# An expert's last 128 tokens in a retention and mixture-of-experts kernel: first layer with the weights stationary instead of the tokens

## The chip, the cores and the metric

The kernel runs on one core of one Trainium2 chip. The metric is device time in microseconds (us) of one execution. The kernel before takes 399.38 us, the median of 3 runs (399.12 to 399.86).

## The reference

Retention attention runs over 4 sequences of 768 steps with 8 heads of 64 features. Its output is one row of 512 features for each of 3072 tokens. A gate then sends every token to one of 8 experts, and each expert is two matrix products with a relu between them.

```python
def _attn_ref(q, k, v):
    ...
    for t in range(S):
        state = gamma[None, :, None, None] * state + np.einsum('bhd,bhe->bhde', k[:, :, t], v[:, :, t])
        y[:, :, t] = scale * np.einsum('bhd,bhde->bhe', q[:, :, t], state)

def _moe_ref(x, w_gate, w1, w2):       # x: 3072 x 512, w1: 8 x 512 x 1024, w2: 8 x 1024 x 512
    ...
    for e in range(E):
        mask = expert_idx == e
        xe = x[mask]
        h = np.maximum(xe @ w1[e], 0.0)
        ye = h @ w2[e]
        out[mask] = gate_w[mask, None] * ye
```

## The kernel before, in words

**Stages.** The first part computes the retention output chunk by chunk (24 chunks of 128 tokens), gates the tokens, and scatters them into DRAM, sorted by expert. The second part, `moe_main`, goes through the experts. Expert 0 is handled in two pieces. Its first 320 tokens are computed while the last chunks of the first part still run (`early_pieces`, L793 and L812). Its last tokens, up to 128 of them, are computed in `late_block` (L899 to L960), which is the first thing in `moe_main` and the place of the change. Experts 1 to 7 follow in a loop (first layer L1009, second layer L1034 or, for the last expert, L1032), each with a fixed capacity of tokens, 452 for expert 1.

**Precision.** Every operand of an expert's product is split into a high part and a low part, both of type fp32r (`whi`, `wlo` for weights; `xh`, `xl` or the two planes of `xhl1` for tokens; `hh`, `hl` or the two planes of `hT` for the features between the layers). A product is the sum of three: high times high, low weight times high, high weight times low. So a 512 x 512 piece of first-layer weights costs 4 blocks of 128 input features (kd) times 3 products.

**A matmul's two operands.** TensorE loads one operand of up to 128 x 128, the stationary one (LDWEIGHTS, engine PEld in the profile), and then streams the other, the moving one, of up to 512 columns (MATMUL, engine PE). The output has one partition for each stationary column.

**The late block.** `hidden(i, part)` computes the first layer for half i of the 1024 features between the layers. The token block `xhl1[:, x, kd, :]` (128 x 128) is stationary and 512 weight columns move, so `hn` (PSUM) has tokens on its partitions: 12 matmuls of 512 columns for each half, in two parts of 6. ACT applies the relu into `hs` (L914). The second layer contracts over the features, so they have to lie on the partitions: `turned(i)` makes four 128 x 128 TensorE transposes into `ht` (L919), and ACT and DVE cut the result into the high and low planes of `hT` (L921, L922). `result(i, part)` is the second layer (L928): `hT` stationary, 512 columns of the second-layer weights moving, 24 matmuls summed in `pys[0]`. `put_rows` (L881) weighs the rows and POOL scatters them to the output (L738).

**What sets the order.** The scheduler is off here (`manual_schedule`): each engine runs its instructions in the order in which the code issues them. Between the steps for expert 0 the late block prepares the 452 tokens of expert 1, in four pieces j of 128 (the last of 68): `prep(j, "turn")` is a transpose on DVE (L753), "high" a cast on ACT (L760), "low" a subtraction on DVE (L767). Behind these, on ACT and DVE, stands the split of the second quarter of expert 1's weights (`split`, L132 and L133), then the fetch of the fourth quarter on SP's queue (`fetch(1, 3)`, L124, which refills a buffer freed by the split), then DVE's weighing of expert 0's first tokens (L894) and their scatters on POOL. PSUM tiles with tag "ph" come from a pool of three, shared by `hn`, `ht` and the `ph` of the later experts.

Of the kernel before, what the change touches and what calls it, by code (L numbers as in the profile page):

```python
# [9 lines left out]
F32 = mybir.dt.float32  # L10
# [3 lines left out]
AF = mybir.ActivationFunctionType  # L14
ALU = mybir.AluOpType
# [3 lines left out]
E, DM, F = 8, 512, 1024  # L19
N = B * S  # L20
P = 128
# [11 lines left out]
KD = DM // P  # L33
# [792 lines left out]
def moe_main(ctx, tc, wparts, fetch, split, xhl1, Z0, ident, buf, xg, fetch_rows, expert_at, mask7, slot_marks, natural, overflow,  # L826
             last_meta, token_index, out):
    nc = tc.nc
# [4 lines left out]
    yp = pool("yp", 2)  # L833
    ps_h = pool("ps_h", 3, space=PS)
# [14 lines left out]
    def marks(e):  # L849

        n = blocks[e]
        sidx[e], gw[e] = slot_marks[e % 3]
        nc.vector.scalar_tensor_tensor(out=sidx[e][:, 0:n], in0=xg.bitcast(I32)[:, 0:n, P], scalar=4 * ROWS,
                                       in1=mask7[:, e - 1, 0:n], op0=ALU.bitwise_and, op1=ALU.bitwise_or)
        nc.vector.tensor_copy(out=gw[e][:, 0:n], in_=xg[:, 0:n, P + 1:P + 2])

    def prep_x(e, j, engine, steps=("turn", "high", "low")):
        if "turn" in steps:
            if j == 0:
                xs[e] = [xp.tile([P, KD, CMAX], F32R, name=n) for n in ("xh", "xl")]  # L860
                if e not in natural and e > 1:
                    marks(e)
            turn_slices(nc, xt[j % 2], xg, 4 * j, widths[e][j], 0)
        args = xt[j % 2], 4 * j, widths[e][j], 0
        if "high" in steps:
            cut_high(nc, xs[e][0], *args)
        if "low" in steps:
            cut_low(nc, engine, *xs[e], *args)

    def put_rows(e, py, j):  # L870
        w = widths[e][j]
        index, meta = natural[e]
        yo = yp.tile([P, DM], F32, name="yo")

        parts = (slice(0, 2), slice(2, 4)) if e == E1 and j == len(widths[e]) - 1 else (slice(0, 4),)
        for i, k in enumerate(parts):
            args = dict(out=sliced(yo[:w, :])[:, k], in_=featured(py[:w, :])[:, k])
            if i:
                nc.scalar.activation(func=AF.Copy, scale=meta[:w, j, 1:2], **args)
            else:  # L880
                nc.vector.tensor_scalar(in0=args["in_"], out=args["out"], scalar1=meta[:w, j, 1:2], scalar2=None,  # L881
                                        op0=ALU.mult)
        scatter_rows(tc, out, index[:w, j:j + 1], yo[:w, :], "rows")
# [7 lines left out]
    def weigh(e, j):  # L891
        a, b = 4 * j, min(4 * j + 4, blocks[e])
        z = Zs[e][:, a:b].rearrange("p j k r -> p j (k r)")
        nc.vector.tensor_tensor(out=z, in0=z, in1=gw[e][:, a:b].broadcast_to([P, b - a, P]), op=ALU.mult)  # L894

    def put_slices(e, j):
        scatter_rows(tc, out_slices, sidx[e][:, j:j + 1], Zs[e][:, j].rearrange("p k r -> p (k r)"), "rows")

    def late_block():  # L899

        hs = [yp.tile([P, DM], F32, name="hs", tag="yo") for _ in range(2)]
        hT = yp.tile([P, 2, KF, P], F32R, name="hT", tag="Z")
        hn = {}

        def hidden(i, part):
            whi, wlo = wparts[0, i]
            if part == 0:
                hn[i] = ps_h.tile([P, DM], F32, name="hn", tag="ph")
            for kd in range(2 * part, 2 * part + 2):
                for n, (a, x) in enumerate(((whi, 0), (wlo, 0), (whi, 1))):  # L910
                    nc.tensor.matmul(out=hn[i], lhsT=xhl1[:, x, kd, :], rhs=a[:, kd, :],
                                     start=(kd == 0 and n == 0), stop=(kd == KD - 1 and n == 2))
            if part:
                nc.scalar.activation(out=hs[i], in_=hn[i], func=AF.Relu)  # L914

        def turned(i):
            t = ps_h.tile([P, 4, P], F32, name="ht", tag="ph")
            for j in range(4):
                nc.tensor.transpose(out=t[:, j, :], in_=hs[i][:, j * P:(j + 1) * P], identity=ident)  # L919
            hi, lo = [hT[:, n, 4 * i:4 * i + 4, :] for n in range(2)]  # L920
            nc.scalar.copy(out=hi, in_=t)  # L921
            nc.vector.tensor_tensor(out=lo, in0=t, in1=hi.bitcast(F32), op=ALU.subtract)  # L922

        def result(i, part):
            whi, wlo = wparts[0, 2 + i]
            for f in range(2 * part, 2 * part + 2):
                for n, (a, h) in enumerate(((whi, 0), (wlo, 0), (whi, 1))):
                    nc.tensor.matmul(out=pys[0], lhsT=hT[:, h, 4 * i + f, :], rhs=a[:, f, :],  # L928
                                     start=(i + f == 0 and n == 0), stop=(i == 1 and f == 3 and n == 2))

        prep = lambda j, *steps: prep_x(1, j, nc.vector, steps)
        hidden(0, 0)
        hidden(0, 1)
        prep(0, "turn")
        prep(1, "turn")
        prep(0, "high")
        prep(1, "high")
        prep(0, "low")
        hidden(1, 0)
        turned(0)  # L940
        prep(1, "low")
        prep(2, "turn")
        hidden(1, 1)
        prep(2, "high")
        result(0, 0)
        turned(1)
        prep(2, "low")
        prep(3, "turn", "high", "low")
        marks(1)
        for i in range(2):  # L950
            split(1, 1, i, nc.vector)
        fetch(1, 3)
        for j in range(-(-NJ0 // 4)):
            weigh(0, j)
        result(0, 1)
        for j in range(4):
            put_slices(0, j)
        result(1, 0)
        result(1, 1)
        put_rows(0, pys[0], 0)  # L960

    with tc.manual_schedule():

        nc.vector.memset(pys[1][:, CAPS[1]:], 0.0)
        late_block()
        for e in range(1, E):
            halves = ((0, nc.vector), (1, nc.vector))
# [5 lines left out]
            hs = []  # L973
# [29 lines left out]
            for f in range(KF):  # L1003
                fo = (f % 4) * P
                ph = ps_h.tile([P, DM], F32, name="ph")
                n = 0
                for a, x in ((0, xh), (1, xh), (0, xl)):
                    for kd in range(KD):
                        nc.tensor.matmul(out=ph[:, :cap], lhsT=wparts[e, f // 4][a][:, kd, fo:fo + P],  # L1009
                                         rhs=x[:, kd, :cap], start=(n == 0), stop=(n == 3 * KD - 1))  # L1010
# [5 lines left out]
                                               in1=hh[:, :cap].bitcast(F32), op0=ALU.max, op1=ALU.subtract)  # L1016
# [3 lines left out]
            for k in range(steps):  # L1020
# [3 lines left out]
                n = 0  # L1024
                for f in range(KF):
                    whi, wlo = wparts[e, 2 + f // 4]
                    hh, hl = hs[f]
                    for a, x in ((whi, hh), (wlo, hh), (whi, hl)):
# [4 lines left out]
                        else:  # L1033
                            nc.tensor.matmul(out=py[:, :cap], lhsT=a[:, f % 4, k * P:(k + 1) * P],  # L1034
                                             rhs=x[:, :cap], **se)
# [137 lines left out]
```

## Time and profile before

| | |
|---|---|
| median of 3 runs | 399.38 us (399.12 to 399.86) |
| the profiled execution | 400.06 us, with a span of 398.3 us from its first to its last instruction |
| mean granted TensorE clock | 0.995 |
| PE matmul instructions | 3236, busy 98% of the span |
| DVE, POOL, ACT busy | 60%, 46%, 36% |
| first matmul of the late block (L911) | 133.01 us after the start of the span |
| first matmul of expert 1 (L1009) | 145.00 us |

PE is TensorE's matmul, PEld its load of the stationary operand, DVE is VectorE, ACT ScalarE, POOL GpSimd, and SP the engine that issues most transfers. In a row of the timeline stand the start, the length, the engine, the line of the kernel, the operation, output and inputs by their names in the program, the form and the count; in square brackets how long the engine was idle before and what ended that. In a row of grouped instructions stand count, busy us, mean ns of one, and the idle time before them. Matmuls are pipelined and their ends are modelled, so the pace is read from their starts. The profile writes fp32r operands of TensorE as f32.

### The profile page before, as it was taken

What the parts mean: (1) busy time and instruction counts of PE and PEld (TensorE: products, weight loads), DVE (VectorE), ACT (ScalarE), POOL (GpSimd) and SP (SyncE); (2) the same over time, 40 slices, a digit from 0 to 9 for tenths busy, and PEclk for the clock granted to TensorE, in tenths of its full rate; (3) what the DMA queues carried; (4) which work ended last, traced back from release to release, by engine and by line L of the source; (5) the groups of instructions that cost most, each with busy time, mean ns of one, the idle gap of its engine ahead of it and who ended that gap; (6) DMA issues with size and microseconds to landing.
All of it is one profiled execution on the core that took longest, in us unless ns stands there. A gap on an engine that the chain in (4) does not pass through costs nothing. (4 is left out here: it accounts for less than half of the span.)

```text
span 398.3 us, 8240 instructions
## 1 busy us (share of the span) xinstructions
PE 390.3 (98%) x3236; PEld 356.5 (89%) x3236; DVE 240.3 (60%) x468; ACT 142.4 (36%) x249; POOL 185.2 (46%) x176
## 2 busy tenths in 40 slices
PE   8999999999999999999999999999999999999994
PEld 4888878787899889999999999999999999999972
DVE  3555757685744578573866477477737657665310
ACT  2224435224411455531542344054334416423100
POOL 1647959655260517200584077028406813740741
PEclk9999999999999999999999999999999999999998
DMA  8999999975058839547452755465564647430111
GB/s 273 422 419 420 418 416 420 324 297 149 2 216 174 327 117 305 214 167 162 166 182 92 190 183 213 84 209 165 177 152 157 234 83 232 146 133 0 54 47 48
DMA packets 42316, 81.53 MB, mean 205 GB/s; under 512 B 4444, under 2 KB 18144, under 8 KB 39844
## 3 DMA queue, kind: packets, MB, share of 16 engines
q1 hardware_dynamic: 36768, 67.46, 51.2%
q0 software_dynamic: 5360, 13.49, 9.1%
q8 instruction: 26, 0.43, 0.4%
q14 instruction: 14, 0.11, 0.1%
q10 hardware_dynamic: 148, 0.04, 0.1%
HBM read 65.90 MB, written 15.68 MB: 205 GB/s over the span
## 5 line engine op out<-in xcount | busy, mean ns | idle before, releaser
L738 POOL DMA_INDIRECT out<-Z,sidx x90 | 104.9, 1165 | 138.8 <-DVE Z L894 113.5
L133 DVE TENSOR_TENSOR wlo<-raw,whi 128x1024 fp32r<-128x1024 f32 x54 | 65.5, 1215 | 14.1 <-ACT whi L132 13.8
L132 ACT CAST whi<-raw 128x1024 fp32r<-128x1024 f32 (+1 forms) x72 | 67.3, 950 | 7.3 <-DMA raw<-w 7.3
L1034 PE MATMUL py<-hl,whi 128*128 128x452 f32 (+5 forms) x192 | 67.0, 349 | 0.0
L1034 PE MATMUL py<-hh,wlo 128*128 128x452 f32 (+5 forms) x192 | 66.8, 348 | 0.0
L1034 PE MATMUL py<-hh,whi 128*128 128x452 f32 (+5 forms) x192 | 66.8, 348 | 0.0
L1014 ACT ACTIVATE hh<-ph 128x452 fp32r<-128x452 f32 (+6 forms) x56 | 28.3, 507 | 81.5 <-PE ph L1009 81.5
L1009 PE MATMUL ph<-xh,wlo 128*128 128x452 f32 (+6 forms) x224 | 50.1, 345 | 0.0
L1009 PE MATMUL ph<-xh,whi 128*128 128x452 f32 (+6 forms) x224 | 50.1, 345 | 0.0
L1009 PE MATMUL ph<-xl,whi 128*128 128x452 f32 (+6 forms) x224 | 50.0, 345 | 0.0
L1015 DVE SCALAR_TENSOR_TENSOR hl<-ph,hh 128x452 fp32r<-128x452 f32 (+6 forms) x56 | 32.0, 574 | 29.7 <-ACT hh L1014 29.2
L1009 PEld LDWEIGHTS ph<-xh,whi 128*128 128x128 f32 x224 | 40.8, 188 | 0.8
L1009 PEld LDWEIGHTS ph<-xh,wlo 128*128 128x128 f32 x224 | 40.8, 188 | 0.8
L1009 PEld LDWEIGHTS ph<-xl,whi 128*128 128x128 f32 x224 | 40.7, 188 | 0.7
L1034 PEld LDWEIGHTS py<-hh,wlo 128*128 128x128 f32 x192 | 36.0, 188 | 0.8
L1034 PEld LDWEIGHTS py<-hl,whi 128*128 128x128 f32 x192 | 36.0, 188 | 0.7
L1034 PEld LDWEIGHTS py<-hh,whi 128*128 128x128 f32 x192 | 36.0, 188 | 0.7
L251 DVE TENSOR_TENSOR Sb<-sp,cs 128x512 f32<-128x512 f32 x48 | 30.8, 684 | 7.4 <-PE sp L248 7.4
L760 ACT CAST xh<-buf 128x512 fp32r<-128x512 f32 (+7 forms) x26 | 14.3, 556 | 56.5 <-DVE buf L753 56.5
L133 POOL TENSOR_TENSOR wlo<-raw,whi 128x512 fp32r<-128x512 f32 (+1 forms) x18 | 24.9, 1403 | 12.7 <-ACT whi L132 10.5
L738 POOL DMA_INDIRECT x_sorted<-xrow,KEY x24 | 24.2, 1010 | 13.1 <-issue 6.5
L889 DVE STREAM_TRANSPOSE Z<-py 128x416 f32<-128x416 f32 (+3 forms) x24 | 15.0, 626 | 24.4 <-PE py L1034 24.4
(163 smaller groups left out, 535.3 us busy)
## 6 DMA issues: line engine op xcount, KB each, us to landing
raw<-w SPq DMA_DIRECT2D x32, 1024.0 KB, 5.6
qkv_w<-qkv SPq DMA_DIRECT2D x12, 1024.0 KB, 18.3
qkv_t<-qkv SPq DMA_DIRECT2D x7, 1024.0 KB, 17.8
qkv_t<-qkv SPq DMA_DIRECT2D x8, 512.0 KB, 6.8
buf<-x_sorted SPq DMA_DIRECT2D x12, 211.2 KB, 4.8
x_sorted<-cs SPq DMA_DIRECT2D x6, 260.0 KB, 5.6
buf<-x_sorted SPq DMA_DIRECT2D x8, 195.0 KB, 4.7
out<-Z,sidx POOLq DMA_INDIRECT x90
```

What stands on the lines that cost most here:

```text
L132: nc.scalar.copy(out=hi[:, h], in_=raw[:, h])
L133: engine.tensor_tensor(out=lo[:, h], in0=raw[:, h], in1=hi[:, h].bitcast(F32), op=ALU.subtract)
L251: nc.vector.tensor_tensor(out=Sb[:, r], in0=sps[r], in1=causal.unsqueeze(1).broadcast_to([P, NP, C]), op=ALU.mult)
L738: sc = tc.nc.gpsimd.indirect_dma_start(out=dst, out_offset=bass.IndirectOffsetOnAxis(ap=index, axis=0), in_=rows, in_offset=None, bounds_c ...
L760: nc.scalar.copy(out=xh[:, :, c0:c0 + w], in_=xt[:, :, t0:t0 + w])
L889: nc.vector.transpose(out=Zs[e][:, 0:nb, k, :], in_=py[:, 0:32 * nb].rearrange("p (j c) -> p j c", c=32))
L1009: nc.tensor.matmul(out=ph[:, :cap], lhsT=wparts[e, f // 4][a][:, kd, fo:fo + P], rhs=x[:, kd, :cap], start=(n == 0), stop=(n == 3 * KD - 1))
L1014: nc.scalar.activation(out=hh[:, :cap], in_=ph[:, :cap], func=AF.Relu)
L1015: nc.vector.scalar_tensor_tensor(out=hl[:, :cap], in0=ph[:, :cap], scalar=0.0, in1=hh[:, :cap].bitcast(F32), op0=ALU.max, op1=ALU.subtract)
L1034: nc.tensor.matmul(out=py[:, :cap], lhsT=a[:, f % 4, k * P:(k + 1) * P], rhs=x[:, :cap], **se)
```

## The change

In the first layer of the late block the operands change places. A 128 x 128 piece of the weights is stationary and the 128 tokens move. The output `t` then has features on its partitions and tokens along its columns, which is the form that the second layer takes as its stationary operand. The transposes, `hs` and `turned` go; the relu moves into the two instructions that cut the features into their high and low planes (an activation on ACT, a max-and-subtract on DVE). `hidden(i)` is one piece now, and stands in other places between the preparation steps of expert 1.

```diff
-        hs = [yp.tile([P, DM], F32, name="hs", tag="yo") for _ in range(2)]
         hT = yp.tile([P, 2, KF, P], F32R, name="hT", tag="Z")
...
-        def hidden(i, part):
+        def hidden(i):
             whi, wlo = wparts[0, i]
-            if part == 0:
-                hn[i] = ps_h.tile([P, DM], F32, name="hn", tag="ph")
-            for kd in range(2 * part, 2 * part + 2):
-                for n, (a, x) in enumerate(((whi, 0), (wlo, 0), (whi, 1))):
-                    nc.tensor.matmul(out=hn[i], lhsT=xhl1[:, x, kd, :], rhs=a[:, kd, :],
-                                     start=(kd == 0 and n == 0), stop=(kd == KD - 1 and n == 2))
-            if part:
-                nc.scalar.activation(out=hs[i], in_=hn[i], func=AF.Relu)
-
-        def turned(i):
             t = ps_h.tile([P, 4, P], F32, name="ht", tag="ph")
+            products = [(a, x, kd) for a, x in ((whi, 0), (wlo, 0), (whi, 1)) for kd in range(KD)]
             for j in range(4):
-                nc.tensor.transpose(out=t[:, j, :], in_=hs[i][:, j * P:(j + 1) * P], identity=ident)
+                for n, (a, x, kd) in enumerate(products):
+                    nc.tensor.matmul(out=t[:, j, :], lhsT=a[:, kd, j * P:(j + 1) * P], rhs=xhl1[:, x, kd, :],
+                                     start=(n == 0), stop=(n == len(products) - 1))
             hi, lo = [hT[:, n, 4 * i:4 * i + 4, :] for n in range(2)]
-            nc.scalar.copy(out=hi, in_=t)
-            nc.vector.tensor_tensor(out=lo, in0=t, in1=hi.bitcast(F32), op=ALU.subtract)
+            nc.scalar.activation(out=hi, in_=t, func=AF.Relu)
+            nc.vector.scalar_tensor_tensor(out=lo, in0=t, scalar=0.0, in1=hi.bitcast(F32), op0=ALU.max,
+                                           op1=ALU.subtract)
...
-        hidden(0, 0)
-        hidden(0, 1)
         prep(0, "turn")
         prep(1, "turn")
+        hidden(0)
         prep(0, "high")
         prep(1, "high")
         prep(0, "low")
-        hidden(1, 0)
-        turned(0)
         prep(1, "low")
         prep(2, "turn")
-        hidden(1, 1)
+        hidden(1)
         prep(2, "high")
         result(0, 0)
-        turned(1)
         prep(2, "low")
```

On PE, at the end of the first half and the start of the second, these rows stand in the kernel before: matmuls of 512 columns with `xhl1` stationary, four transposes (L919) in between, and the second layer (L928).

```order
L911 MATMUL hn<-whi,xhl_1869 128x512
L919 MATMUL ht<-cs,hs 128x128 x4
L911 MATMUL hn<-whi,xhl_1869 128x512
L911 MATMUL hn<-wlo,xhl_1869 128x512
L911 MATMUL hn<-whi,xhl_1869 128x512 x2
L911 MATMUL hn<-wlo,xhl_1869 128x512
L911 MATMUL hn<-whi,xhl_1869 128x512
L928 MATMUL py_2230<-whi,hT 128x512
```

In the changed kernel PE has matmuls of 128 columns, in runs of four or eight, from the last of expert 0's early tokens (L812) to the second layer (now L920); the first rows of that stretch and its last ones are these.

```order
L812 MATMUL acc_1811<-hl_1735,whi 128x320
L909 MATMUL ht<-xhl_1869,whi 128x128 x4
L909 MATMUL ht<-xhl_1869,wlo 128x128 x4
L909 MATMUL ht<-xhl_1869,whi 128x128 x8
...
L909 MATMUL ht<-xhl_1869,whi 128x128 x8
L909 MATMUL ht<-xhl_1869,wlo 128x128 x4
L909 MATMUL ht<-xhl_1869,whi 128x128 x4
L920 MATMUL py_2230<-whi,hT 128x512
```

Where 24 matmuls of 512 columns and 8 transposes stood, there are 96 matmuls of 128 columns, each with a load of its own, and no transpose.

On DVE, over the same stretch, the step for the first half moves ahead of expert 1's low parts (L767), and that for the second half stands behind the turn of piece 2 (L753), as before.

```order
 L753 STREAM_TRANSPOSE buf<-buf 128x4x4x32 x2
-L767 TENSOR_TENSOR xl<-buf,xh 128x4x128
-L922 TENSOR_TENSOR hT<-ht,hT 128x512
-L767 TENSOR_TENSOR xl<-buf,xh 128x4x128
-L753 STREAM_TRANSPOSE buf<-buf 128x4x4x32
-L922 TENSOR_TENSOR hT<-ht,hT 128x512
+L913 SCALAR_TENSOR_TENSOR hT<-ht,hT 128x512
+L767 TENSOR_TENSOR xl<-buf,xh 128x4x128 x2
+L753 STREAM_TRANSPOSE buf<-buf 128x4x4x32
+L913 SCALAR_TENSOR_TENSOR hT<-ht,hT 128x512
```

DVE's number of steps for the two halves stays at two, and the first of them (now L913) now stands in front of the low parts of pieces 0 and 1.

More of the change, by code (lines that the diff above doesn't have):

```diff
@@ L899, in late_block @@
     def late_block():
-        hs = [yp.tile([P, DM], F32, name="hs", tag="yo") for _ in range(2)]
         hT = yp.tile([P, 2, KF, P], F32R, name="hT", tag="Z")
-        hn = {}
-        def hidden(i, part):
+        def hidden(i):
             whi, wlo = wparts[0, i]
-            if part == 0:
-                hn[i] = ps_h.tile([P, DM], F32, name="hn", tag="ph")
-            for kd in range(2 * part, 2 * part + 2):
-                for n, (a, x) in enumerate(((whi, 0), (wlo, 0), (whi, 1))):
-                    nc.tensor.matmul(out=hn[i], lhsT=xhl1[:, x, kd, :], rhs=a[:, kd, :],
-                                     start=(kd == 0 and n == 0), stop=(kd == KD - 1 and n == 2))
-            if part:
-                nc.scalar.activation(out=hs[i], in_=hn[i], func=AF.Relu)
-        def turned(i):
             t = ps_h.tile([P, 4, P], F32, name="ht", tag="ph")
+            products = [(a, x, kd) for a, x in ((whi, 0), (wlo, 0), (whi, 1)) for kd in range(KD)]
             for j in range(4):
-                nc.tensor.transpose(out=t[:, j, :], in_=hs[i][:, j * P:(j + 1) * P], identity=ident)
+                for n, (a, x, kd) in enumerate(products):
+                    nc.tensor.matmul(out=t[:, j, :], lhsT=a[:, kd, j * P:(j + 1) * P], rhs=xhl1[:, x, kd, :],
+                                     start=(n == 0), stop=(n == len(products) - 1))
             hi, lo = [hT[:, n, 4 * i:4 * i + 4, :] for n in range(2)]
-            nc.scalar.copy(out=hi, in_=t)
-            nc.vector.tensor_tensor(out=lo, in0=t, in1=hi.bitcast(F32), op=ALU.subtract)
+            nc.scalar.activation(out=hi, in_=t, func=AF.Relu)
+            nc.vector.scalar_tensor_tensor(out=lo, in0=t, scalar=0.0, in1=hi.bitcast(F32), op0=ALU.max,
+                                           op1=ALU.subtract)
         def result(i, part):
```

## The prediction, made blind

> **What bounds the kernel now.** I read the page's busy shares first, then the busy time by stretch, then TensorE's timeline around the change. Here is part 1 of the page.
>
> ```profile
> PE 390.3 (98%) x3236; PEld 356.5 (89%) x3236; DVE 240.3 (60%) x468; ACT 142.4 (36%) x249; POOL 185.2 (46%) x176
> ```
>
> PE is busy in 98% of the span. That is an average, and matmul ends are modelled, so I ask for the busy time by stretch. 133 to 145 us is the block that the change rewrites; the next two stretches are all the later experts; the last is the tail. The columns are length, busy time of PE, PEld, DVE, ACT and POOL with counts, granted clock, DMA share and GB/s.
>
> ```profile
> 133.00:145.00 12.00, 12.00 (x58) 9.84 (x57) 7.66 (x16) 6.22 (x11) 4.56 (x2) 1.00 0.68 238
> 145.00:184.00 39.00, 39.00 (x192) 35.69 (x191) 27.91 (x43) 16.77 (x23) 11.96 (x11) 1.00 0.61 188
> 184.00:391.00 207.00, 207.00 (x1126) 202.45 (x1125) 123.70 (x182) 73.69 (x108) 95.82 (x82) 1.00 0.48 147
> 391.00:398.30 7.30, 1.38 (x6) 0.67 (x4) 0.48 (x1) 0.47 (x1) 1.01 (x1) 0.73 0.10 27
> ```
>
> In the block and in everything behind it PE fills the whole stretch at a granted clock of 1.00. No engine and no transfer makes TensorE wait after 133 us, so nothing later can swallow a delay or pass on less than a gain: a microsecond more or less of PE time in the block moves the end by a microsecond. The tail of 7.3 us hangs on PE's last matmuls and moves with them. So the forecast is a sum over PE's starts, and then a look at whether the other engines still keep up.
>
> The starts matter, not the durations: a matmul's row is longer than the distance to the next start, since they are pipelined. This is PE's timeline in and around the block (start, length, line, form, count).
>
> ```profile
> 126.11 0.31 PE L812 MATMUL acc<-hh,wlo 128*128 128x320 f32 x1
> ...
> 127.58 0.31 PE L812 MATMUL acc<-hl,whi 128*128 128x320 f32 x1
> ...
> 133.01 0.41 PE L911 MATMUL hn<-whi,xhl 128*128 128x512 f32 x1
> ...
> 136.91 0.39 PE L911 MATMUL hn<-whi,xhl 128*128 128x512 f32 x1
> 137.14 0.60 PE L919 MATMUL ht<-cs,hs 128*128 128x128 f32 x4
> 137.50 0.47 PE L911 MATMUL hn<-whi,xhl 128*128 128x512 f32 x1
> 137.81 0.39 PE L911 MATMUL hn<-wlo,xhl 128*128 128x512 f32 x1
> ...
> 138.96 0.40 PE L928 MATMUL py<-whi,hT 128*128 128x512 f32 x1
> ...
> 140.36 0.60 PE L919 MATMUL ht<-cs,hs 128*128 128x128 f32 x4
> 140.72 0.48 PE L928 MATMUL py<-whi,hT 128*128 128x512 f32 x1
> 141.03 0.40 PE L928 MATMUL py<-wlo,hT 128*128 128x512 f32 x1
> ...
> 145.00 0.98 PE L1009 MATMUL ph<-xh,whi 128*128 128x452 f32 x4
> 145.82 0.98 PE L1009 MATMUL ph<-xh,wlo 128*128 128x452 f32 x4
> ```
>
> Ten matmuls of 320 columns lie between 126.11 and 127.58, 0.147 us each; four of 452 columns take 0.82 us, 0.205 each; eighteen of 512 columns lie between 133.01 and 137.14, 0.2294 each. From 320 to 512 columns that is 82.4 ns for 192 columns, 0.429 ns a column, with about 10 ns left over per matmul.
>
> **The change part by part.** *Removed from PE.* The 24 first-layer matmuls of 512 columns with the tokens stationary, and the 8 transposes (two rows of x4). From 133.01 to 138.96 stand all 24 matmuls and the first four transposes: 5.95 us. The other four transposes: from 140.36 to 141.03 is 0.67, of which one 512-column matmul is 0.23, so 0.44. Together 6.39 us. (The four transposes of the first group come out alike: 137.14 to 137.81 less 0.23 is 0.44, 0.11 each.)
>
> *Added to PE.* 96 matmuls with a 128x128 weight piece stationary and 128 token columns moving. The multiplications are the same in number, 24 x 512 = 96 x 128 columns, but there are now 96 weight loads where there were 24. So what matters is whether a load still hides behind the stream before it. These are rows of the weight loads: first by form (line, form, count, busy, mean ns of one), then two in order of time.
>
> ```profile
> L911 PEld LDWEIGHTS hn<-whi,xhl 128*128 128x128 f32 x16 | 3.0, 188 | 0.6
> L1032 PEld LDWEIGHTS py<-whi,hh 128*104 128x104 f32 x8 | 1.3, 168 | 0.5
> L332 PEld LDWEIGHTS L<-xT,wgs 128*32 128x32 f32 x96 | 1.9, 108 | 1.9 <-issue 1.0 <-DVE Sb L251 0.8
> L919 PEld LDWEIGHTS ht<-cs,hs 128*128 128x128 f32 x8 | 1.0, 140 | 0.3
> ...
> 137.47 0.19 PEld L911 LDWEIGHTS hn<-whi,xhl 128*128 128x128 f32 x1
> 137.58 0.19 PEld L911 LDWEIGHTS hn<-wlo,xhl 128*128 128x128 f32 x1
> 137.81 0.19 PEld L911 LDWEIGHTS hn<-whi,xhl 128*128 128x128 f32 x1
> ```
>
> A load grows from 108 ns at 32 columns to 168 at 104 and 188 at 128: (188 - 108) / 96 = 0.833 ns a column. 128 columns then occupy the load path for 107 ns, and 81 ns of the 188 are a fixed latency that the next instruction can overlap. The loads at 137.58 and 137.81 start where the matmul ahead of them starts (the matmul at 137.81, and the one whose row of 137.50 is 0.08 too long), so one load at a time runs behind one matmul, and a matmul starts when its own load is in and the matmul ahead has streamed. At 512, 452 and 320 columns the stream (229, 205, 147 ns) covers the 107. At 128 columns the stream would be 147 - 192 x 0.429 = 65 ns, and does not. So the load sets the pace: 107 ns at least, 117 if the 10 ns left over at each wide matmul come on top. No row has this form in steady state. The nearest rows are the transposes, also 128 x 128 with 128 columns moving, at 110 ns each, and the two loads at 137.47 and 137.58, 110 ns apart. I take 109. 96 x 0.109 = 10.46 us; the ends are 96 x 0.107 = 10.27 and 96 x 0.117 = 11.23.
>
> The Trainium skill has a rule that speaks for less: the page TensorE: Matmul & The Clock Gate, section Back-to-back issue gap, gives about 81 ns per matmul for a sustained stream of loads and matmuls at 128 columns. By that rule the 96 would take an estimated 7.8 us and the time would be 400.8; the transposes here, at 110 ns, do not agree with it.
>
> *Sum on PE.* 10.46 - 6.39 = +4.07 us (ends +3.9 and +4.8). The 24 second-layer matmuls (L928) stay as they are. The block would end at 145.00 + 4.07 = 149.07 on the scale of this trace.
>
> *ACT, DVE.* ACT loses two evictions with relu (600 ns each) and its two copies become the relu; DVE's two subtractions become a max-and-subtract of the same size. Neither engine bounds anything here, so this removal earns nothing. But both are in-order queues, and what is moved matters: the first hidden half is now ready only after 48 matmuls, and behind its ACT and DVE steps stand the pieces of expert 1's tokens that PE needs straight after the block. These are their rows (turn is L753, high L760, low L767).
>
> ```profile
> 135.98 0.60 ACT L914 ACTIVATE hs<-hn 128x512 f32<-128x512 f32 x1 [2.35 <-PE hn L911]
> 140.34 0.62 ACT L760 CAST xh<-buf 128x512 fp32r<-128x512 f32 x1 [0.58 <-DVE buf L753]
> 143.43 0.42 ACT L760 CAST xh<-buf 128x272 fp32r<-128x272 f32 x1 [1.84 <-DVE buf L753]
> 141.62 0.69 DVE L922 TENSOR_TENSOR hT<-ht,hT 128x512 fp32r<-128x512 f32 x1 [1.31 <-ACT hT L921]
> 142.22 0.68 DVE L767 TENSOR_TENSOR xl<-buf,xh 128x512 fp32r<-128x512 f32 x1
> 142.82 0.57 DVE L753 STREAM_TRANSPOSE buf<-buf 128x384 f32<-128x384 f32 x1
> 143.88 0.44 DVE L767 TENSOR_TENSOR xl<-buf,xh 128x272 fp32r<-128x272 f32 x1 [0.49 <-ACT xh L760]
> ```
>
> The low parts of pieces 0 and 1 now wait on DVE behind the first half, until about 140; PE needs them after 150. The second half leaves PE at 133.0 + 10.46 = 143.5, and I allow 0.3 for the last matmul's drain. Then ACT: relu 143.8 to 144.4, high of piece 2 to 145.0. DVE: the half's low part to 145.1, low of piece 2 to 145.8, turn of piece 3 to 146.3; ACT's high of piece 3 to 146.8; DVE's last low to 147.2. PE comes to the second half after twelve 512-column matmuls at 0.23, at 146.3: 1.2 us to spare. It needs the last high piece at 149.07: 2.3 to spare; the last low piece eight matmuls of 452 columns later (1.64), at 150.7: 3.5 to spare. If ACT or DVE ran later than that, PE would stall by the excess, and nothing behind would take it back. Expert 1's next weight pieces are split on ACT and DVE behind these, some 3 us later than now, while PE needs them 4 us later; the fetch on SP's queue that a freed raw buffer lets go moves alike. POOL's scatters of expert 0 wait for DVE's weighing and start some 3 us later; they have the whole of expert 1 to drain. I cost all of this at nothing.
>
> **The rivals.** *The stream sets the pace* (the other side: not slower). If a load hid fully behind a 65 ns stream, the 96 would take 6.24 us and the block would be 0.15 shorter: 399.2 us, no change. It decides at 6.39 / 96 = 66.6 ns a matmul; below that the change wins. For it: the array sees the same number of columns, and the transposes' loads of 140 ns (59 beyond the fixed 81) show that a 128-column load can be faster. Against it: those are loads of another kind, and every first-layer load here is 188. Chance 0.03.
>
> *Loads start early.* If a load could start ahead of the matmul before it, the pace would lie between 65 and 109, at the middle 87: 8.35 us, +1.96, 401.3. The load rows against it start within 0.01 us of the matmul ahead. Chance 0.05. The 81 ns of the Trainium skill (TensorE: Matmul & The Clock Gate, Back-to-back issue gap) would lie in this case.
>
> *Load and stream add up.* 107 + 65 = 172 ns: 16.5 us, +10.1, 409.5. Against it: at 320 columns the spacing of 147 is far under 107 + 137 (320 x 0.429). Chance 0.02.
>
> *Narrow moving tiles stream slower in this data type.* These operands are fp32r, and no fp32r matmul of the trace moves fewer than 320 columns. Plain f32 ones at 128 columns are dearer, as these two rows show.
>
> ```profile
> 101.62 1.09 PE L287 MATMUL Y<-Sb,vs 128*64 128x128 f32 x16
> 102.65 0.66 PE L304 MATMUL tr<-cs,xT 128*128 128x128 f32 x4
> ```
>
> The code issues eight products there (L287) and the trace counts sixteen matmuls: each product runs as two. They lie in 1.03 us, two at a time on the two halves of the array's columns, so a product takes at most 1.03 / 4 = 0.26 us. If narrow fp32r fell back to that, the 96 would take 24.7 us: +18.3, 417.7. Against it: the wide fp32r matmuls run as one each, and nothing in their rows bends toward 320 columns. Chance 0.04.
>
> *A late queue.* If the second half's low part were late on DVE by one step more than I count, say by a split of 1.2 us, it would eat the 1.2 us to spare; a stall of 1 us more gives 404.5. Chance 0.02.
>
> **How the numbers follow.** The sum is made on the profiled execution: span 398.3 and 1.76 around it make 400.06 us, 0.68 above the median of the three runs, 399.38 (399.12 to 399.86). So this execution would become 404.1 and the median 399.38 + 4.07 = 403.45, say 403.5. The likeliest case, the load as the pace, has 0.84; the stream 0.03, early loads 0.05, the plain sum 0.02, slow narrow tiles 0.04, a late queue 0.02. The bounds of the load's pace give 403.3 to 404.2; the scatter of the runs shown adds 0.3 below and 0.5 above; the 107 comes from rounded means and may be 3 ns off (0.3 us below), and a late step would add some tenths above. So 402.7 to 405.0. It leaves out the four rivals that end elsewhere, 0.14 together, and a little of the main case. The 0.2% that a measurement of this kernel can tell from no change is 0.8 us. Only the first rival ends inside that band, 0.02, or beyond it if the stream ran under 58 ns a matmul, 0.01. All other cases are slower: 0.97.
>
> **What would show it right or wrong.** Right: in the changed kernel's PE timeline the block's first-layer matmuls start 0.107 to 0.117 us apart, 96 of them in about 10.5 us; every one of their loads starts with the matmul ahead and has its 188 ns; the first matmul of expert 1 starts about 4.1 us later than 145.00; PE stays busy through all the later stretches with lengths unchanged, and the tail is again 7.3 us. ACT's and DVE's last pieces for expert 1 end before PE asks for them. Wrong in the price: a pace near 65 or 87 ns, or over 0.17, with the block's length off by 96 times the difference. Wrong in the cover: idle time of PE before L928's second half or before expert 1's first or ninth matmul, named as waiting for DVE or ACT. Wrong in the premise: later stretches shorter than before, so that part of the 4 us is taken back.

## The result, and the profile after

The changed kernel takes 403.9 us, the median of 5 runs (403.45 to 404.5), beside 399.34 us for the kernel before in the same session (5 runs, 399.12 to 399.86). The ratio is 1.0109 with a 95% interval of 1.0097 to 1.012: 4.56 us slower, where +4.07 was forecast; 403.9 lies inside the forecast range of 402.7 to 405.0. Medians and ranges are of all runs, while ratios and their intervals, here and below, leave out runs in a slower state. The profiled execution has a span of 402.1 us.

These are the rows of PE's timeline in the changed kernel that answer to those shown of before (start, length, line, form, count). The first layer is now L909, the second L920, expert 1's first layer L997.

```profile
132.63 0.58 PE L909 MATMUL ht<-xhl,whi 128*128 128x128 f32 x4
133.04 0.61 PE L909 MATMUL ht<-xhl,wlo 128*128 128x128 f32 x4
133.49 1.06 PE L909 MATMUL ht<-xhl,whi 128*128 128x128 f32 x8
...
142.87 0.61 PE L909 MATMUL ht<-xhl,whi 128*128 128x128 f32 x4
143.32 0.45 PE L920 MATMUL py<-whi,hT 128*128 128x512 f32 x1
143.60 0.39 PE L920 MATMUL py<-wlo,hT 128*128 128x512 f32 x1
...
145.93 0.63 PE L920 MATMUL py<-whi,hT 128*128 128x512 f32 x2
146.40 0.39 PE L920 MATMUL py<-wlo,hT 128*128 128x512 f32 x1
146.63 0.63 PE L920 MATMUL py<-whi,hT 128*128 128x512 f32 x2
...
148.96 0.98 PE L997 MATMUL ph<-xh,whi 128*128 128x452 f32 x4
```

From 132.63 to 143.32 lie the 96 narrow matmuls: 10.69 us, 0.1114 each. From there to 148.96 lie the 24 of the second layer: 5.64. The block is 16.33 us long where it was 11.99, so 4.34 more. The busy time by stretch shows that PE has no gap behind the block either (length; busy time of PE, PEld, DVE, ACT and POOL with counts; clock, DMA share, GB/s).

```profile
132.63:148.96 16.33, 16.33 (x122) 15.26 (x121) 8.70 (x17) 5.64 (x9) 4.48 (x2) 1.00 0.50 177
148.96:188.00 39.04, 39.04 (x192) 35.81 (x191) 27.13 (x42) 15.90 (x22) 12.08 (x11) 1.00 0.66 188
188.00:395.00 207.00, 207.00 (x1127) 202.38 (x1126) 123.63 (x182) 73.63 (x108) 95.80 (x82) 1.00 0.48 147
395.00:402.10 7.10, 1.25 (x6) 0.59 (x4) 0.48 (x1) 0.47 (x1) 1.01 (x1) 0.74 0.10 27
```

PE fills every stretch up to 395 us, at a clock of 1.00, as before. From the first matmul of expert 1 to the start of the last matmul (395.86 here, 391.99 before) pass 246.90 us where it was 246.99, so nothing behind the block takes the 4.34 back. Between the two profiled executions the span grew by 3.8 us and not by 4.34: this block begins at 132.63 and not at 133.01, 0.38 less, and from its end to the end of the span it is 0.16 less (253.14 beside 253.30). How soon the block begins differs from run to run: 132.71, 132.08 and 131.88 in three of the executions below. The median's 4.56 less 4.34 leaves 0.2 us, which is within the scatter of the five runs.

The loads of the new matmuls, by form (count, busy us, mean ns of one):

```profile
L909 PEld LDWEIGHTS ht<-xhl,whi 128*128 128x128 f32 x64 | 7.9, 192 | 0.0
L909 PEld LDWEIGHTS ht<-xhl,wlo 128*128 128x128 f32 x32 | 4.2, 192 | 0.0
```

And two rows of them in order of time:

```profile
132.99 0.53 PEld L909 LDWEIGHTS ht<-xhl,wlo 128*128 128x128 f32 x4
133.43 0.97 PEld L909 LDWEIGHTS ht<-xhl,whi 128*128 128x128 f32 x8
```

From 132.99 to 133.43 four loads start, so they lie 0.11 us apart like the matmuls, and PEld is busy without a gap. A load lasts 192 ns here (188 among the wide matmuls of L920). The first load of a low weight starts at 132.99 and its matmul's row at 133.04: the matmul's row begins while the row of its load still has some 0.14 us to run. I read the rest of that wait as part of the matmul's row, so the pace has to be read from the distances between starts and not from lengths.

### The profile page after: what moved, and what is told of

Same layout as the page of the kernel before. It is cut to its first block, busy times and chain, and to the rows that moved or that the text cites. A ratio compares the mean times of both kernels' runs of the same rounds, so it can differ in the third digit from the quotient of the medians.

```text
span 402.1 us, 8364 instructions
## 1 busy us (share of the span) xinstructions
PE 394.6 (98%) x3300; PEld 362.1 (90%) x3300; DVE 241.0 (60%) x468; ACT 140.9 (35%) x247; POOL 185.2 (46%) x176
## 5 line engine op out<-in xcount | busy, mean ns | idle before, releaser
L997 PE MATMUL ph<-xh,wlo 128*128 128x452 f32 (+6 forms) x224 | 50.1, 345 | 0.0
L997 PE MATMUL ph<-xh,whi 128*128 128x452 f32 (+6 forms) x224 | 50.1, 345 | 0.0
L997 PE MATMUL ph<-xl,whi 128*128 128x452 f32 (+6 forms) x224 | 50.0, 345 | 0.0
L997 PEld LDWEIGHTS ph<-xh,whi 128*128 128x128 f32 x224 | 40.8, 188 | 0.9
L997 PEld LDWEIGHTS ph<-xh,wlo 128*128 128x128 f32 x224 | 40.7, 188 | 0.8
L997 PEld LDWEIGHTS ph<-xl,whi 128*128 128x128 f32 x224 | 40.7, 188 | 0.7
L133 POOL TENSOR_TENSOR wlo<-raw,whi 128x512 fp32r<-128x512 f32 (+1 forms) x18 | 24.8, 1401 | 12.9 <-ACT whi L132 10.7
```

What stands on the lines that cost most here:

```text
L133: engine.tensor_tensor(out=lo[:, h], in0=raw[:, h], in1=hi[:, h].bitcast(F32), op=ALU.subtract)
```

## The experiments

All of them start from the changed kernel unless it is said otherwise. They ran in three sessions. The first four ran beside a kernel before that took 411.38 us (29 runs, 408.94 to 415.68) and their late blocks began some 8 us later than the blocks above; with them I compare blocks, not totals. The last eight ran in two sessions, with 399.47 and 399.25 us for the kernel before. A block is the distance from the first matmul of the late block to the first of expert 1.

**Is it the load?** My theory was that a load of 128 columns sets the pace. The first rival: a narrow fp32r stream runs at half speed, which at 128 columns would come to the same 107 ns. The second: a load and its matmul cost 0.111 us together, whatever their sizes. The first experiment halves the load.

```diff
-nc.tensor.matmul(out=t[:, j, :], lhsT=a[:, kd, j * P:(j + 1) * P], rhs=xhl1[:, x, kd, :],
+nc.tensor.matmul(out=t[0:64, j, :], lhsT=a[:, kd, j * P:j * P + 64], rhs=xhl1[:, x, kd, :],
...
```

> The changed kernel with only the first 64 of each 128 weight columns loaded: 96 matmuls with 64-column loads and 128 token columns moving; half of the features between the layers is left out, and the second layer contracts over 64 rows with as many matmuls of 512 columns. My theory: the load takes 64 x 0.833 = 53 ns, less than the stream, and the stream of about 65 ns sets the pace: 96 x 0.065 = 6.2 us, 4.4 less than the changed kernel, near 399.4. First rival (slow narrow stream) and second rival (fixed cost): the pace stays at 0.107 to 0.111 and the time at the changed kernel's 403.9.

First its PE timeline at the ends of the layer and the start of expert 1, then its loads by form.

```profile
140.89 0.40 PE L909 MATMUL ht<-xhl,whi 128*64 128x128 f32 x4
141.13 0.40 PE L909 MATMUL ht<-xhl,wlo 128*64 128x128 f32 x4
...
146.74 0.50 PE L920 MATMUL py<-whi,hT 64*128 64x512 f32 x1
...
152.53 0.67 PE L997 MATMUL ph<-xh,whi 128*128 128x452 f32 x2
```

```profile
L909 PEld LDWEIGHTS ht<-xhl,whi 128*64 128x64 f32 x64 | 4.5, 134 | 0.0
```

The 96 matmuls take 5.85 us, 0.061 each, with the same 128 columns moving. Both rivals fall: the narrow stream runs at full speed, and there is no fixed 0.111. The block is 11.64 us (140.89 to 152.53), and the total 411.87 beside 411.38 of the kernel before (ratio 1.0, 0.9966 to 1.0034). No difference was expected; the interval is 1.4 us wide to each side, so the evidence is the pace and not the total.

**The other half of the cross.** Full loads, half the columns moving.

```diff
 for j in range(4):
+    for c in range(0, P, 64):
...
-        rhs=xhl1[:, x, kd, :]
+        rhs=xhl1[:, x, kd, c:c + 64]
```

> The changed kernel with the 128 token columns moved in two halves: 192 matmuls, each with a full 128x128 weight load and 64 columns moving. My theory (the load of 128 columns, 107 ns, sets the pace): the pace stays at 0.111 us, the first layer takes 192 x 0.111 = 21.3 us against 10.7 now, so about 10.7 us over the changed kernel and 15.2 over the kernel before, near 414.5. First rival (a narrow fp32r stream runs at half speed, 0.83 ns a column, and the load is hidden): 64 columns take 53 to 57 ns, the layer stays at 10.2 to 11 us and the time near 404. Second rival (a fixed cost of 0.111 per load and matmul, whatever their sizes): like my theory, 414.5.

It took 442.27 us (441.08 to 445.9), 30.9 over the kernel before where 15.2 was expected, so it missed every expectation. The stretches of its busy time show why; the column in front of the last two numbers is the granted clock.

```profile
140.75:143.80 3.05, 3.05 (x30) 3.05 (x29) 2.20 (x5) 0.00 (x0) 2.99 (x2) 1.00 1.03 379
143.80:178.81 35.01, 35.01 (x166) 35.01 (x166) 2.51 (x4) 1.62 (x3) 0.00 (x0) 0.50 0.10 31
178.81:181.35 2.54, 2.54 (x7) 2.06 (x8) 1.68 (x3) 1.10 (x2) 0.00 (x0) 0.50 0.00 0
181.35:185.65 4.30, 4.30 (x20) 3.45 (x20) 3.47 (x7) 2.33 (x3) 0.00 (x0) 1.00 0.00 0
```

In the first 3.05 us the matmuls start 0.111 to 0.112 us apart (eight of them from 141.58 to 142.47), as the load theory says: the pace does not go down with the stream. Then the granted clock falls to 0.50 and the pace is 0.213 (four matmuls from 143.83 to 144.68). The full clock comes back 2.5 us after the wide matmuls of the second layer have begun. So the theory held and the time did not, for a reason that none of the three theories had.

**Fewer narrow streams.** Each high weight piece is loaded once, with the high and low token planes side by side as 256 columns; ACT and DVE add the two planes of the result.

```diff
+if n < KD:
+    nc.tensor.matmul(out=t[:, o], lhsT=whi[:, kd, j * P:(j + 1) * P], rhs=xhl1[:, :, kd, :],
+                     start=(n == 0), stop=False, skip_group_check=True)
+else:
+    nc.tensor.matmul(out=t[:, o, 1], lhsT=wlo[:, kd, j * P:(j + 1) * P], rhs=xhl1[:, 0, kd, :],
+                     start=False, stop=(n == 2 * KD - 1), skip_group_check=True)
...
+nc.scalar.copy(out=high, in_=t[:, :, 0])
+nc.vector.tensor_tensor(out=high, in0=t[:, :, 1], in1=high, op=ALU.add)
```

> The changed kernel with the token planes moved together: each high weight piece is loaded once and 256 columns move (high and low tokens side by side), each low weight piece with 128 columns; 64 loads instead of 96; ACT and DVE add the two planes of the result. My theory: 256 columns cost 256 x 0.429 + 10 = 0.120 us and hide the next load, 128 columns cost 0.111: 32 x 0.231 = 7.4 us against 10.7, so 3.3 less than the changed kernel and 1.0 over the kernel before, near 400.4. First rival (narrow streams at 0.83 ns a column): 256 columns cost up to 0.213, the layer 10.4 us, the time near 403.6. The adds cost nothing as long as the second half's low part is there 2.8 us after its last matmul; if not, some tenths more.

The first comparison was too wide to tell (412.79 beside 411.38, ratio 1.0032, 0.9996 to 1.0068), so it ran again in the last session.

> The kernel with 256-column matmuls for the high weights, again, since the first comparison was too wide to tell: block 12.98 us, 1.0 us over the kernel before and 3.3 under the changed one, so 400.4 beside 399.4. A slow narrow stream would have given 403.6.

It took 400.27 us beside 399.25 (ratio 1.0023, 1.0014 to 1.0032). Its timeline, in the second of the two comparisons:

```profile
132.65 0.66 PE L913 MATMUL ht<-xhl,whi 128*128 128x256 f32 x4
133.15 0.56 PE L916 MATMUL ht<-xhl,wlo 128*128 128x128 f32 x4
133.54 0.68 PE L913 MATMUL ht<-xhl,whi 128*128 128x256 f32 x4
...
139.97 0.45 PE L931 MATMUL py<-whi,hT 128*128 128x512 f32 x1
...
145.63 0.57 PE L1008 MATMUL ph<-xh,whi 128*128 128x452 f32 x2
```

The layer takes 7.32 us (7.4 expected) and the block 12.98, 1.0 over before. It saves 3.35 of the changed kernel's 4.34 us, but it does not beat the kernel before: 64 loads of 107 ns are 6.85 us, more than the 6.39 that were removed.

**The removed part alone.** The kernel before without its transposes.

```diff
-t = ps_h.tile([P, 4, P], F32, name="ht", tag="ph")
-for j in range(4):
-    nc.tensor.transpose(out=t[:, j, :], in_=hs[i][:, j * P:(j + 1) * P], identity=ident)
+t = hs[i].rearrange("p (j t) -> p j t", j=4)
```

> The kernel before without its 8 transposes: the relu output is cut into high and low parts as it lies, so the second layer gets tokens where features should be. My theory: PE loses 8 x 0.110 = 0.88 us on its path and nothing covers them, so 0.9 us less than before, near 398.5. Rival: the transposes fill time in which PE would wait for ACT's relu and DVE's low part anyway, so less than 0.3 us is won, 399.1 or more.

The first comparison (410.67 beside 411.38, ratio 0.9971, 0.9934 to 1.0007) could not tell 0.9 from 0.3, but its block of 11.44 us lay between the two. It ran again.

> The kernel before without its 8 transposes, again: the first look gave a block of 11.44 us where 11.99 less 0.88 is 11.11, with PE waiting for ACT and DVE three times in the second layer. My theory now: the transposes' time was in part cover for the chain of relu, high and low part; 0.5 to 0.6 us less than before. Rival: those waits were of that run; 0.9 less.

398.86 us beside 399.25, ratio 0.9987 (0.9978 to 0.9997), and again a block of 11.44: 0.55 us shorter, not 0.88. The totals alone, 0.1 to 0.9 us less by the interval, can't tell these two apart; the block in both profiles does. The first of these two fences shows the waits of its second layer's loads on PEld, the second ACT's timeline around them.

```profile
138.35 0.30 PEld L926 LDWEIGHTS py<-whi,hT 128*128 128x128 f32 x2 [0.21 <-DVE hT L920]
140.74 0.19 PEld L926 LDWEIGHTS py<-whi,hT 128*128 128x128 f32 x1 [0.24 <-ACT hT L919]
141.47 0.30 PEld L926 LDWEIGHTS py<-whi,hT 128*128 128x128 f32 x2 [0.43 <-DVE hT L920]
```

```profile
138.14 0.60 ACT L914 ACTIVATE hs<-hn 128x512 f32<-128x512 f32 x1 [0.57 <-PE hn L911]
139.55 0.62 ACT L760 CAST xh<-buf 128x512 fp32r<-128x512 f32 x1 [0.81 <-DVE buf L753]
140.07 0.62 ACT L919 CAST hT<-hs 128x512 fp32r<-128x512 f32 x1
```

With the transposes gone, PE reaches the second half before ACT does: ACT's cast for it stands in the queue behind a cast for expert 1, which waits 0.81 us for DVE. DVE's low part for that half follows ACT's cast, which is the wait of 0.43. So 0.33 of the transposes' 0.88 us had covered that chain.

**Is the cover real?** I had costed ACT's and DVE's later steps at nothing. The second half's low part is done at 144.84 in the changed kernel, and PE first uses it at 146.63.

```profile
144.15 0.69 DVE L913 SCALAR_TENSOR_TENSOR hT<-ht,hT 128x512 fp32r<-128x512 f32 x1 [2.85 <-ACT hT L912]
```

First the changed kernel ran once more, without any edit.

> The changed kernel once more, beside the next three. My theory: 96 matmuls at 0.111 us, the late block 16.3 us long as in its first profile, and 1.1% over the kernel before (about 4.4 us). A rival that the first result's excess over 4.07 us is a later wait: PE idle behind the block.

403.61 us beside 399.47, ratio 1.0103 (1.0086 to 1.012); the block is 16.35 us (132.71 to 149.06) and PE is busy through it and behind it. The rival, a later wait, falls. Then DVE's step is repeated, to use the cover up.

```diff
-nc.vector.scalar_tensor_tensor(out=lo, in0=t, scalar=0.0, in1=hi.bitcast(F32), op0=ALU.max, op1=ALU.subtract)
+for _ in range(3 if i else 1):
+    nc.vector.scalar_tensor_tensor(out=lo, in0=t, scalar=0.0, in1=hi.bitcast(F32), op0=ALU.max, op1=ALU.subtract)
```

> The changed kernel with DVE's step for the second half's low part done three times instead of once, 2 x 0.61 = 1.2 us more on DVE at the place where expert 1's pieces queue behind it. My theory: it is ready 1.8 us before PE uses it and the pieces behind it have 2.6 and 3.7 us to spare, so the cover holds, no idle time on PE, the block 16.3 us as in the changed kernel. Rival (DVE's queue is on the path): up to 1.2 us longer.

403.69 us, block 16.33 us: no change. DVE's three steps took 2.14 us, so 1.45 us of added delay was absorbed. With `range(6 if i else 1)`:

> The same step six times, 5 x 0.61 = 3.05 us more. My theory: the cover of 1.8 us is used up and PE waits 3.05 - 1.8 = 1.2 us in front of the second half of the second layer, block 17.5 us; expert 1's pieces, 3 us later, then still come in time. Rival (an own slack behind takes it): no change.

405.92 us, ratio 1.0171 (1.0154 to 1.0188), 2.3 us over the changed kernel. DVE's row, and the PE rows around the wait:

```profile
143.40 4.32 DVE L914 SCALAR_TENSOR_TENSOR hT<-ht,hT 128x512 fp32r<-128x512 f32 x6 [2.85 <-ACT hT L912]
```

```profile
145.66 0.40 PE L921 MATMUL py<-wlo,hT 128*128 128x512 f32 x1
147.77 0.73 PE L921 MATMUL py<-whi,hT 128*128 128x512 f32 x2 [1.72 <-DVE hT L914]
...
150.21 0.98 PE L998 MATMUL ph<-xh,whi 128*128 128x452 f32 x4
```

PE waits where it was expected to, but longer. The five added steps cost (4.32 - 0.69) / 5 = 0.726 us each, not the 0.61 by which steps on different tiles follow each other in the changed kernel (144.15 and 144.76). The likely reason, not tested, is that each writes the same tile as the one before it. 3.63 us less the cover of 1.79 is 1.84, and the block is 18.33, 2.0 over. Most of the rest is at the restart: PE begins 0.05 us after DVE ends, and its next two matmuls take 0.57 us where the two before took 0.47. The cover was as large as read; the step was mis-sized. Nothing behind took the stall back: from the block's end to the end of the span it is 253.2 us, as in the repeated run of the changed kernel.

**The clock.** The fall of the clock with 64 columns asked how near the changed kernel is to it. At the 0.429 ns a column that the wide matmuls gave, an estimate, its 128 columns stream 55 of every 111 ns.

```diff
-nc.tensor.matmul(out=t[:, j, :], lhsT=a[:, kd, j * P:(j + 1) * P], rhs=xhl1[:, x, kd, :],
+nc.tensor.matmul(out=t[:, j, 0:96], lhsT=a[:, kd, j * P:(j + 1) * P], rhs=xhl1[:, x, kd, 0:96],
...
```

> The changed kernel with 96 of the 128 token columns moving (the last 32 tokens of the block are left out), full 128-column loads. Load sets the pace: 0.111 us still, the block 16.3 us, no change from the changed kernel, as long as the granted clock stays at 1.0. With 64 columns moving the clock fell to 0.5 after 3 us, where the stream was 64 x 0.429 = 27 of every 111 ns; at 128 columns (55 of 111) it stayed. If the bound lies under 41 of 111 (37%) the clock stays; if it lies above, the pace is 0.213 after 3 us, 27 matmuls at 0.111 and 69 at 0.213, 17.7 us for the layer and 7 us more in all.

411.01 us (408.04 to 411.41), 7.4 over the changed kernel of the same session, with a quarter of the token columns left out. The mean granted clock of its four runs is 0.978 to 0.986, beside 0.995 to 0.999 for the changed kernel, so the fall is in every run, and how long it lasts differs. The stretches of the profiled one:

```profile
133.04:138.53 5.49, 5.49 (x52) 5.49 (x50) 2.69 (x6) 0.48 (x1) 4.36 (x2) 1.00 0.85 316
138.53:148.43 9.90, 9.90 (x48) 9.90 (x48) 2.42 (x4) 1.51 (x3) 0.00 (x0) 0.50 0.28 107
148.43:152.18 3.75, 3.75 (x10) 2.55 (x11) 2.30 (x6) 2.26 (x4) 0.00 (x0) 0.50 0.00 0
152.18:155.71 3.53, 3.53 (x16) 2.47 (x16) 3.40 (x4) 1.05 (x2) 0.16 (x1) 1.00 0.02 5
```

The clock falls 5.5 us into the layer and stays at 0.50 for 13.65 us, so it also slows the first ten matmuls of the second layer. With 112 columns (`0:112` in the same places):

> As with 96 columns, now 112 of the 128 token columns move (the last 16 tokens of the block are left out). The stream is 48 of 111 ns, 43%. 37% made the clock fall and 50% did not. The load theory gives 0.111 us a matmul and the changed kernel's time, 403.7, if the clock holds; if it falls as with 96 columns, 6 to 7 us more, near 411. I lean to the fall.

403.47 us, ratio 1.0099 (1.0084 to 1.0115): the clock held in all four runs (means of 0.995 to 0.998), against my lean. And twice the length with 128 columns:

```diff
 for j in range(4):
+    for _ in range(2):
...
         for n, (a, x, kd) in enumerate(products):
```

> The changed kernel with every first-layer product group done twice (the same sums, written again): 192 matmuls of 128 columns with full loads instead of 96. If the clock goes by the share of the time in which columns stream (55 of 111 ns, as in the changed kernel), it stays at 1.0 however long the stretch is: 10.7 us more than the changed kernel, 414.3. If it is only the shortness of the stretch that saved the changed kernel, the clock falls to 0.5 some 10 us in: the remaining matmuls at 0.213, 8 us more or beyond, 422 or more.

414.6 us (414.17 to 415.54), ratio 1.0385 (1.0368 to 1.0402). One row for each of the two, the one with 112 columns first, over their first layers:

```profile
132.09:142.77 10.68, 10.68 (x98) 10.68 (x97) 5.13 (x10) 2.13 (x4) 4.46 (x2) 1.00 0.70 262
```

```profile
131.98:153.39 21.41, 21.41 (x194) 21.41 (x193) 4.72 (x9) 2.02 (x4) 4.29 (x2) 1.00 0.35 131
```

Of the columns that I tried, 64 and 96 (25% and 37% of the time streaming, by the same estimate) drop the clock within 3.1 and 5.5 us, 112 and 128 (43% and 50%) do not, for 10.7 and for 21.4 us. The kernels with 96 and with 112 columns ran in different sessions, so where between them the bound lies, and whether it stays there, is not shown. A rival is the transfers, since both falls come where a burst of them ends (a DMA share of 1.03, then 0.10, with 64 columns). With twice the length the share also falls, from 0.92 before 137.0 us to 0.14 in the next 3 us, and is 0.00 from 146 us on, and the clock holds; that rival falls too. The second row also measures the disputed cost by itself: 96 more of the same matmuls cost 10.72 us in the trace.

## Why the prediction was right, point by point

*No slack behind the block.* Right. PE stays without a gap to its last matmuls, and the stall that was added came out at the end in full.

*Removed, 6.39 us.* Right as a sum over the starts of before: 11.99 less the 5.60 of the second layer. The kernel without transposes adds one thing that I had not seen: taken away alone, the 0.88 would have given 0.55, since the transposes covered 0.33 us of the chain on ACT and DVE. In the changed kernel this chain is covered by twelve second-layer matmuls, so the sum stood.

*Added, 96 x 0.109.* The mechanism was right: the load sets the pace. The size was a little low: 0.1114, so 10.69 us and not 10.46, 0.23 more. The other 0.04 of the block is the first second-layer matmul, 0.28 long where the others are 0.23. 4.07 + 0.23 + 0.04 = 4.34. The last 0.2 us of the measured 4.56 belongs to no term; it lies within the scatter of the runs. "Every one of their loads ... has its 188 ns" was off: they last 192, and the recorded start of a matmul can't be taken as the start of its stream.

*The cover on ACT and DVE, costed at nothing.* Right, and conservative: I counted 1.2 us to spare for the second half and it was 1.79, since PE uses the low part two matmuls after it comes to that half. A delay of 1.45 us was absorbed, and one of 3.63 showed 2.0 us of stall. Expert 1's last high and low pieces were ready at 146.38 and 146.86, and PE came to them at 148.96 and 150.60.

*The rivals.* The stream as the pace (0.061 was measured with half loads) would have needed half the load time. Loads that start early and the 81 ns for sustained 128-column matmuls that the Trainium skill gives (TensorE: Matmul & The Clock Gate, Back-to-back issue gap) do not hold for these operands: 111 ns, and the measurement decides. A slow narrow fp32r stream is refuted by 0.061, and a load and a stream that add up would have given 172 ns where 111 was measured. A late queue did not come: PE has no idle time in the block.

*What the prediction lacked.* It took the clock of 1.00 for granted: no row of narrow matmuls with full loads stood behind it, and no rival. That the clock held at 128 columns was luck as far as the prediction goes: with a quarter fewer token columns in the block the same change cost 11.5 us against the kernel before (411.01 beside 399.47), where the changed kernel of that session cost 4.1.

## What to carry to other kernels

Swapping stationary and moving operands keeps the multiplications and multiplies the loads: count the loads, and compare one load (0.833 ns a column, 107 ns for 128 fp32r columns here) with the stream it must hide behind (0.43 ns a column); below some 250 moving columns, an estimate from these two, the load is the pace. Transposes at 0.11 us each were cheap beside that, and part of their time was covering another chain. Narrow streams behind full loads can also cost the clock, as they did here at 64 and 96 columns, so read the granted clock of the stretch and not only PE's busy share.

## What the runs showed of the hardware that was not expected

TensorE's granted clock halved while PE and PEld were both busy without a gap, when the streaming columns took an estimated 25% or 37% of the time (27 or 41 of 111 ns), and not at 43% or 50%. At a clock of 0.50 the pace that the loads set went from 0.111 to 0.213 us. The fall came 3.1 and 5.5 us after the narrow stretch began, and full clock came back 2.54 and 3.75 us after wide matmuls resumed, 37.55 and 13.65 us after the fall. The Trainium skill (TensorE: Matmul & The Clock Gate, section HAM oscillation — how this bites in real kernels) ties the lower clock to gaps of TensorE between bursts; here there was no gap in the rows, only a small share of streaming.

With half loads, 64 columns at 134 ns, 128 columns stream at 0.061 us a matmul, 6 ns over the estimated 55 of the columns, where wide matmuls carry 10.
